# Attention and a squared-ReLU FFN in one kernel: fixed engine orders, and attention in pairs of chunks

## The chip, the cores and the metric

The kernel runs on one core of one Trainium2 chip. The metric is the device time of one execution in microseconds (us). The core has five engines that run side by side, each with a queue of its own that it works through in order: TensorE (PE, matrix products and transposes, into PSUM), VectorE (DVE), ScalarE (ACT), GpSimd (POOL), and SyncE (SP), which here issues all DMAs. [...]a bank holds 128 x 512 numbers of 32 bits.

## The reference

Sliding-window attention, whose result is the input of a feed-forward network (FFN):

```python
# q, k, v: [8, 8, 576, 64] (batch, head, position, head_dim), float32
scores = q @ k.transpose(0, 1, 3, 2) / 8
mask = (0 <= rel) & (rel < 64)              # rel = query position - key position
attn = softmax(where(mask, scores, -1e9))
x = (attn @ v).transpose(0, 2, 1, 3).reshape(4608, 512)
h = maximum(x @ w_in, 0)                    # w_in:  [512, 2048]
out = h * h @ w_out                         # w_out: [2048, 512]
```

## The kernel before

The 4608 tokens are cut into 36 chunks of 128 (two blocks of 64 positions, all eight heads), and the FFN into nine groups of four chunks (512 tokens). Everything that PE reads is 16-bit.

**A chunk of attention** has these steps:
- `load` (L176): three DMAs bring k, q and v in 32 bits into buffers of the pool `stage` (17 of them, shared with the weights), and POOL casts each one and makes a copy of v shifted by 64 partitions (L193 to L200).
- `transposes` (L202, chunks 0 to 11): PE transposes k and q into one PSUM bank, DVE copies k to `kT` (L213) together with a halo, the last 64 keys of the chunk before (L210), and ACT copies q to `qT` (L215). From chunk 12 on it is `transposes_k` (L218), and q is transposed by a DMA from SBUF to SBUF (L234).
- `scores` (L237): 16 small matmuls into two PSUM banks, one exponential on ACT and one minimum with a mask on DVE for each bank (L251, L253). The mask holds 65504 or 0, so the minimum keeps a value or clears it.
- `values` (L256): 16 matmuls for the two halves of the heads, each half into a bank of its own, with a reciprocal of the sum (L267) and a multiplication by it (L268) on DVE for each half.
- `to_xT` (L273): the result is transposed by PE and copied by DVE (chunks 0 to 11), or transposed by a DMA (L281, chunks 12 on).

**The FFN.** `ffn_up_chunk` (L326) computes h for one chunk in four quarters of w_in's columns (chunks 0 to 7). `ffn_up` (L309) does a group in 16 steps of four matmuls (L315), with a ReLU on ACT (L319) and the square on DVE (L320). `ffn_out` (L354) is the second product for group 0. `ffn_out_seven` (L373), for the groups 1 to 8, does it with seven half-size products in place of eight, in 14 steps, with sums of h on DVE (L387), and takes sums of w_out (L147 to L164).

**The order.** Work is handed out as a list of small steps. A front works through chunks 0 to 7 with their FFN (L446 to L467). Then comes a loop over g = 1 to 9 (L468): round g holds the output product of group g-1, the up product of group g, the attention of group g+1 and the loads of group g+2, mixed by `weave` (L16). A scheduler then orders the instructions of each engine by its own model of when they will be ready; only those given to `keep_in_program_order` (`pin`, L68), the loads and casts of the front, keep their order. The attention pool `ps_att` has four buffers of one bank.

Of the kernel before, what the change touches and what calls it, by code (L numbers as in the profile page):

```python
# [15 lines left out]
def weave(*streams):  # L16

    keyed = []
    for s, (steps, lo, hi) in enumerate(streams):
        n = len(steps)  # L20
        for i, step in enumerate(steps):
            keyed.append((lo + (hi - lo) * (i + 0.5) / n, s, i, step))
    keyed.sort(key=lambda e: e[:3])
    return [e[3] for e in keyed]
# [3 lines left out]
def kernel(  # L28
# [22 lines left out]
    NTB = NT // 512  # L51

# [12 lines left out]
    ps_att = ctx.enter_context(tc.tile_pool(name="ps_att", bufs=4, space=bass.MemoryType.PSUM))  # L65

    NFIRST = 8
    pin = tc.keep_in_program_order  # L68
# [3 lines left out]

# [10 lines left out]

    def make_mask(name, first):
        m = const.tile([P, HP * 2, 64], FP16, name=name)
        nc.vector.tensor_copy(out=m[:], in_=base[:].rearrange("p (o r) -> p o r", o=1)  # L90
                              .to_broadcast([P, HP * 2, 64]))
        m = m[:].rearrange("p (a b) r -> p a b r", b=2)
        if first is not None:
            nc.vector.memset(m[0:64, :, first, :], 0.0)
        return m

    mask_first = make_mask("mask_first", 0)
    mask_inner = make_mask("mask_inner", None)
    mask_second = make_mask("mask_second", 1)

    w_in_sb = const.tile([P, DMC, DFF], FP16, name="w_in_sb")
    w_out_sb = const.tile([P, FFC, DM], FP16, name="w_out_sb")

# [8 lines left out]
    def load_w_in():  # L112
        steps = []
        FQ = DFF // 4

        def one(quar, c):
            ws = stage.tile([P, FQ], FP32, name="ws", tag="st")
            pin(nc.sync.dma_start(out=ws[:], in_=moe_w_in[c * P:(c + 1) * P,
                                                          quar * FQ:(quar + 1) * FQ]))
            nc.vector.tensor_scalar(  # L120
                out=w_in_sb[:, c, quar * FQ:(quar + 1) * FQ], in0=ws[:],
                scalar1=W_SCALE, scalar2=None, op0=ALU.mult)

        for quar in range(4):
            for c in range(DMC):
                steps.append(lambda quar=quar, c=c: one(quar, c))
        return steps

    def load_w_out():
        def one(f):  # L130
            ws = stage.tile([P, DM], FP32, name="ws2", tag="st")
            pin(nc.sync.dma_start(out=ws[:], in_=moe_w_out[f * P:(f + 1) * P, :]))
            pin(nc.gpsimd.tensor_copy(out=w_out_sb[:, f, :], in_=ws[:]))

        return [lambda f=f: one(f) for f in range(FFC)]

    GW = 1
    GX = 3
    KH = FFC // 2
    NH = DM // 2
    wb = [const.tile([P, KH, NH], FP16, name=f"wb{i}") for i in range(3)]

    def w_out_sums():  # L147
        def sums(k0, kind):
            ks, kl = slice(k0, k0 + 2), slice(KH + k0, KH + k0 + 2)
            b11, b12 = w_out_sb[:, ks, 0:NH], w_out_sb[:, ks, NH:DM]  # L150
            b21, b22 = w_out_sb[:, kl, 0:NH], w_out_sb[:, kl, NH:DM]
            tt = nc.vector.tensor_tensor
            if kind == 0:
                tt(out=wb[1][:, ks], in0=b22, in1=b12, op=ALU.subtract)
            elif kind == 1:
                tt(out=wb[0][:, ks], in0=wb[1][:, ks], in1=b11, op=ALU.add)
            elif kind == 2:
                tt(out=wb[2][:, ks], in0=b21, in1=wb[0][:, ks], op=ALU.subtract)
            else:
                tt(out=b12, in0=b12, in1=b11, op=ALU.subtract)  # L160

        return ([lambda k0=k0, kind=kind: sums(k0, kind)
                 for kind in range(3) for k0 in range(0, KH, 2)],
                [lambda k0=k0: sums(k0, 3) for k0 in range(0, KH, 2)])  # L164


    xTs = {}
# [6 lines left out]
    q16s, k16s, qTs, kTs, pms, xs = {}, {}, {}, {}, {}, {}  # L174

    def load(i):  # L176

        pin = tc.keep_in_program_order if i < NFIRST else lambda ins: ins
        sts = []
        for (src, nm) in ((k, "k"), (q, "q"), (v, "v")):  # L180
            st = stage.tile([P, H, D], FP32, name=f"{nm}_st", tag="st")
            b0, j0 = divmod(2 * i, NB)
            if j0 + 1 < NB:
                pin(nc.sync.dma_start(
                    out=st[:], in_=src[b0, :, 64 * j0:64 * j0 + P, :].rearrange("h p d -> p h d")))
            else:
                pin(nc.sync.dma_start(
                    out=st[0:64], in_=src[b0, :, 64 * j0:S, :].rearrange("h p d -> p h d")))
                pin(nc.sync.dma_start(
                    out=st[64:P], in_=src[b0 + 1, :, 0:64, :].rearrange("h p d -> p h d")))  # L190
            sts.append(st)
        k16s[i] = st16.tile([P, H * D], FP16, name="k16", tag="k16")
        pin(nc.gpsimd.tensor_copy(out=k16s[i][:], in_=sts[0][:].rearrange("p h d -> p (h d)")))  # L193
        q16s[i] = st16.tile([P, H * D], FP16, name="q16", tag="q16")
        pin(nc.gpsimd.tensor_copy(out=q16s[i][:], in_=sts[1][:].rearrange("p h d -> p (h d)")))  # L195
        v_ev, v_od, v_next = v_evs[i % NV], v_ods[i % NV], v_ods[(i + 1) % NV]
        pin(nc.gpsimd.tensor_copy(out=v_ev[:, :, 0:D], in_=sts[2][:]))  # L197
        pin(nc.gpsimd.tensor_copy(out=v_od[64:P, :, 0:D], in_=v_ev[0:64, :, 0:D]))  # L198
        if i + 1 < NCK:
            pin(nc.gpsimd.tensor_copy(out=v_next[0:64, :, 0:D], in_=v_ev[64:P, :, 0:D]))  # L200

    def transposes(i):  # L202
        ps = ps_att.tile([P, 2, HP, P], FP16, name="qkT_ps", tag="ps_a")
        for s, src in enumerate((k16s, q16s)):
            for hp in range(HP):
                nc.tensor.transpose(out=ps[:, s, hp, :], in_=src[i][:, hp * P:(hp + 1) * P],
                                    identity=ident[:])
        kT = attw.tile([P, HP, 192], FP16, name="kT", tag="kT")
        if i > 0:
            nc.vector.tensor_copy(out=kT[:, :, 0:64], in_=kTs[i - 1][:, :, P:192])  # L210
        else:
            nc.vector.memset(kT[:, :, 0:64], 0.0)
        nc.vector.tensor_copy(out=kT[:, :, 64:192], in_=ps[:, 0])  # L213
        qT = attw.tile([P, HP, P], FP16, name="qT", tag="qT", bufs=8)
        nc.scalar.activation(out=qT[:], in_=ps[:, 1], func=AF.Copy, scale=1.0)  # L215
        kTs[i], qTs[i] = kT, qT

    def transposes_k(i):  # L218
        ps = ps_att.tile([P, HP, P], FP16, name="qkT_ps", tag="ps_a")
        for s, src in enumerate((k16s,)):  # L220
            for hp in range(HP):
                nc.tensor.transpose(out=ps[:, hp, :], in_=src[i][:, hp * P:(hp + 1) * P],
                                    identity=ident[:])
        kT = attw.tile([P, HP, 192], FP16, name="kT", tag="kT")
        if i > 0:
            nc.vector.tensor_copy(out=kT[:, :, 0:64], in_=kTs[i - 1][:, :, P:192])
        else:
            nc.vector.memset(kT[:, :, 0:64], 0.0)
        nc.vector.tensor_copy(out=kT[:, :, 64:192], in_=ps[:])
        kTs[i] = kT  # L230

    def transpose_q_dma(i):
        qT = attw.tile([P, HP, P], FP16, name="qT", tag="qT", bufs=8)
        nc.sync.dma_start_transpose(out=qT[:], in_=q16s[i][:])  # L234
        qTs[i] = qT

    def scores(i):  # L237
        sc = [ps_att.tile([P, HP, 2, 64], FP32, name=f"sc{hh}", tag="ps_a") for hh in range(2)]
        for hp in range(HP):
            for blk in range(2):  # L240
                for hh in range(2):
                    r0 = 64 * hh
                    nc.tensor.matmul(  # L243
                        sc[hh][:, hp, blk, :], kTs[i][r0:r0 + 64, hp, 64 * blk:64 * blk + P],
                        qTs[i][r0:r0 + 64, hp, 64 * blk:64 * blk + 64], start=True, stop=True)
        j0 = 2 * i % NB
        mask = mask_first if j0 == 0 else mask_second if j0 + 1 == NB else mask_inner
        pms[i] = []
        for hh in range(2):
            pm = attw.tile([P, HP, 2, 64], FP16, name=f"pm{hh}", tag=f"pm{hh}")  # L250
            nc.scalar.activation(out=pm[:], in_=sc[hh][:], func=AF.Exp,  # L251
                                 scale=1.0 / float(D) ** 0.5)
            nc.vector.tensor_tensor(out=pm[:], in0=pm[:], in1=mask, op=ALU.min)  # L253
            pms[i].append(pm)
# [193 lines left out]
    for s in w_in_steps[:12]:  # L448
        s()
# [63 lines left out]
```

The softmax here doesn't subtract the row's maximum and nothing guards it: scores larger than these inputs give would overflow.

## Time and profile before

| | |
|---|---|
| Median of three runs | 330.17 us (330.02 to 330.44) |
| Span of the profiled execution | 328.2 us |
| Mean granted TensorE clock | 0.987 |
| DMA: bytes moved, packets | 52.98 MB, 148199 |
| POOL waiting for the loads of k (L193) | 81.6 us, 15 waits |

The span runs from the first to the last instruction of one profiled execution; the runs' times contain a little more around it. A group of instructions is shown as line, engine, operation, output<-inputs, shape and count, then its busy time in us and the mean duration of one in ns, then the idle time of the engine just before and what ended it. The slices are 40 equal parts of the span, each digit the busy share in tenths. Durations of neighbouring instructions on one engine overlap, so the time from start to start is shorter than the duration.

### The profile page before, as it was taken

To read this page: it belongs to the slowest core of one execution; us is meant where nothing else is said; L and a number is where in the kernel's file an instruction comes from. 1 tells how busy PE (TensorE), PEld (TensorE's weight loads), DVE (VectorE), ACT (ScalarE), POOL (GpSimd) and SP (SyncE) were. 2 spreads that over 40 slices of the span, in tenths; PEclk is the share of its full clock that TensorE was granted. 3 is DMA by queue.
4 is the path that set the end of the run, shared out by engine and by line. 5 is a ranking of instruction groups with operands and counts; after the bars stand their busy time and mean duration, and the time that the engine had idled before them with its cause. 6 is when DMAs were issued, how large, how long until landed. Compare 5 with 4: busy or idle time off the path is not lost.

```text
span 328.2 us, 8415 instructions
## 1 busy us (share of the span) xinstructions
PE 302.5 (92%) x3334; PEld 205.7 (63%) x3334; DVE 274.7 (84%) x602; ACT 140.4 (43%) x249; POOL 132.6 (40%) x204
## 2 busy tenths in 40 slices
PE   1968989988999999999899999999999999999994
PEld 0357877864575667556565666666656666666683
DVE  2765988999988989898899899999989888876862
ACT  1243557543336543553355345535543544344310
POOL 5038898899907430564065446242822000000000
PEclk9996999999999999999999999999999999999999
DMA  7999989998929545976795788549954101300113
GB/s 196 331 236 222 234 247 373 221 229 208 224 59 248 134 92 155 221 140 132 186 231 113 167 230 187 92 101 277 202 131 115 66 19 32 139 7 2 64 66 128
DMA packets 148199, 52.98 MB, mean 161 GB/s; under 512 B 139456, under 2 KB 139456, under 8 KB 148160
## 3 DMA queue, kind: packets, MB, share of 16 engines
q1 hardware_dynamic: 148160, 52.45, 64.9%
q8 instruction: 26, 0.43, 0.5%
q14 instruction: 13, 0.11, 0.1%
HBM read 36.70 MB, written 9.44 MB: 141 GB/s over the span
## 4 chain that ended last, share of the span: by engine, by line
PE 64%; DVE 25%; ACT 4%; DMA 2%; issue 2%; SPq 2%; ACTq 0%; DVEq 0%
PE hps L315 25%; PE opsD L394 9%; PE opsC L394 8%; PE opsA L394 6%; DVE pm L253 5%; PE hps L336 4%; DVE h L341 4%; DVE h L320 4%; PE av L263 3%; PE opsB L394 3%; PE sc L243 2%; DMA ws<-in_moe_w_in_dram 2%; DVE h L387 2%; ACT hrelu L340 2%; DVE hs L387 2%
## 5 line engine op out<-in xcount | busy, mean ns | idle before, releaser
L315 PE MATMUL hps<-xT,w_in_sb 128*128 128x512 f16 x448 | 114.6, 380 | 3.3 <-DVE h L320 1.8
L319 ACT ACTIVATE hrelu<-hps 128x512 f32<-128x512 f32 x112 | 67.1, 599 | 104.6 <-PE hps L315 95.3
L320 DVE SCALAR_TENSOR_TENSOR h<-hps,hrelu 128x512 f16<-128x512 f32 x112 | 76.6, 684 | 20.7 <-ACT hrelu L319 19.5
L394 PEld LDWEIGHTS <-h 128*128 128x128 f16 x640 | 61.8, 98 | 19.0
L315 PEld LDWEIGHTS <-w_in_sb 128*128 128x128 f16 x448 | 40.7, 98 | 35.8 <-issue 3.3
L193 POOL CAST k<-k_st 128x512 f16<-128x512 f32 x36 | 24.7, 686 | 83.0 <-DMA k_st<-in_k_dram 81.6
L251 ACT ACTIVATE pm<-sc 128x512 f16<-128x512 f32 x72 | 39.0, 597 | 13.8 <-PE sc L243 13.8
L336 PE MATMUL hps<-xT,w_in_sb 128*128 128x128 f16 x512 | 37.8, 226 | 4.9 <-DVE h L341 1.6
L336 PEld LDWEIGHTS <-w_in_sb 128*128 128x128 f16 x512 | 32.1, 101 | 8.1 <-issue 4.6
L394 PE MATMUL opsD<-wb,h 128*128 128x256 f16 x256 | 32.9, 273 | 0.0
L394 PE MATMUL opsA<-w_out_sb,h 128*128 128x256 f16 x256 | 32.7, 273 | 0.0
L253 DVE TENSOR_TENSOR pm<-pm,mask_inner 128x512 f16<-128x512 f16 x56 | 29.7, 544 | 2.8 <-ACT pm L251 2.3
L195 POOL CAST q<-q_st 128x512 f16<-128x512 f32 x36 | 25.2, 699 | 13.4 <-DMA q_st<-in_q_dram 13.3
L340 ACT ACTIVATE hrelu<-hps 128x512 f32<-128x512 f32 x32 | 19.1, 598 | 26.6 <-PE hps L336 23.6
L197 POOL CAST v_ev<-v_st 128x512 f16<-128x512 f32 x36 | 23.5, 653 | 12.9 <-DMA v_st<-in_v_dram 12.2
L394 PEld LDWEIGHTS <-hs 128*128 128x128 f16 x256 | 23.8, 98 | 6.7 <-DVE hs L387 0.5
L268 DVE TENSOR_TENSOR x_sb<-av,rden 128x256 f16<-128x256 f32 x72 | 27.4, 416 | 0.1
L341 DVE SCALAR_TENSOR_TENSOR h<-hps,hrelu 128x512 f16<-128x512 f32 x32 | 21.9, 685 | 6.4 <-ACT hrelu L340 6.3
L200 POOL COPY v_od<-v_ev 64x512 f16<-64x512 f16 x35 | 25.0, 715 | 2.1
L198 POOL COPY v_od<-v_ev 64x512 f16<-64x512 f16 x36 | 24.2, 673 | 2.3
L263 PEld LDWEIGHTS <-pm 128*64 128x64 f16 x576 | 12.9, 110 | 13.4 <-issue 5.7
L263 PE MATMUL av<-v_od,pm 128*64 128x65 f16 x288 | 18.0, 198 | 2.1 <-DVE pm L253 1.4
(63 smaller groups left out, 349.0 us busy)
## 6 DMA issues: line engine op xcount, KB each, us to landing
k_st<-in_k_dram SPq DMA_DIRECT2D x32, 256.0 KB, 3.9
q_st<-in_q_dram SPq DMA_DIRECT2D x32, 256.0 KB, 4.2
v_st<-in_v_dram SPq DMA_DIRECT2D x32, 256.0 KB, 4.4
out_dram<-osb SPq DMA_DIRECT2D x16, 512.0 KB, 3.0
ws<-in_moe_w_in_dram SPq DMA_DIRECT2D x16, 256.0 KB, 5.9
ws<-in_moe_w_out_dram SPq DMA_DIRECT2D x16, 256.0 KB, 5.6
k_st<-in_k_dram SPq DMA_DIRECT2D x8, 128.0 KB, 2.9
q_st<-in_q_dram SPq DMA_DIRECT2D x8, 128.0 KB, 3.1
```

Of the source, the lines that this page charges most:

```text
L195: pin(nc.gpsimd.tensor_copy(out=q16s[i][:], in_=sts[1][:].rearrange("p h d -> p (h d)")))
L251: nc.scalar.activation(out=pm[:], in_=sc[hh][:], func=AF.Exp, scale=1.0 / float(D) ** 0.5)
L253: nc.vector.tensor_tensor(out=pm[:], in0=pm[:], in1=mask, op=ALU.min)
L263: nc.tensor.matmul(av[64 * blk:64 * blk + 64, h % 4, 0:65], pms[i][h % 2][:, h // 2, blk, :], vv[:, h, 0:65], start=True, stop=True)
L268: nc.vector.tensor_tensor(out=x_sb[:, 4 * half:4 * half + 4, :], in0=av[:, :, 0:D], in1=rden[:].to_broadcast([P, 4, D]), op=ALU.mult)
L315: nc.tensor.matmul(hps[:], w_in_sb[:, c, f * P:(f + 1) * P], xT_of(g)[:, c, :], start=(c == 0), stop=(c == DMC - 1))
L319: nc.scalar.activation(out=hrelu[:], in_=hps[:], func=AF.Relu)
L320: nc.vector.scalar_tensor_tensor(out=h2s[g][:, f, :], in0=hps[:], scalar=0.0, in1=hrelu[:], op0=ALU.max, op1=ALU.mult)
L336: nc.tensor.matmul(hps[:, f, :], w_in_sb[:, c, (4 * fq + f) * P:(4 * fq + f + 1) * P], xT_of(g)[:, c, t0:t0 + P], start=(c == 0), stop=(c ...
L340: nc.scalar.activation(out=hrelu[:], in_=hps[:], func=AF.Relu)
L341: nc.vector.scalar_tensor_tensor(out=h2s[g][:, 4 * fq:4 * fq + 4, t0:t0 + P], in0=hps[:], scalar=0.0, in1=hrelu[:], op0=ALU.max, op1=ALU.mult)
L394: nc.tensor.matmul(banks[bank][:, m, :], a[:, k, m * P:(m + 1) * P], w[:, k], start=(first and k == 0 and m == 0), stop=(k == KH - 1), ski ...
```

## The change

All instructions are now issued in program order on every engine (`manual_schedule`). For chunks 0 to 11 and the first FFN group that order comes from a table of some 440 words. Each word is a step: `fk3` fetches k of chunk 3, `kc`, `qc`, `vc`, `vd` cast and shift, `T` transposes, `S` scores, `e` exponential, `m` minimum, `V` values, `n` normalises, `X`/`x` transposes and copies the result, `U2.1` is quarter 1 of the up product of chunk 2 with `r` and `s` its ReLU and square, `fw`/`w` fetch and scale pieces of w_in, `fo`/`o` those of w_out, `O` is the output product, `ws` sums of w_out, `tk`/`tq` transposes by DMA, `h` a halo, `W` matmuls that only keep PE warm.

```diff
+Q_ACT = (0,)
+FIRST = '''
+fk0 fq0 fv0 fw0.0 fw0.1 kc0 fw0.2 qc0 fw0.3 fk1 T0 W4 vc0 fq1 ck0 cq0 vd0 fv1 w0.0 S0 W6 w0.1 ea0
+fw1.0 w0.2 eb0 ma0 mb0 w0.3 V0 W5 fw1.1 kc1 n0 fw1.2 qc1 fw1.3 X0 fk2 T1 x0 vc1 fq2 U0.0 cq1 ck1
...
+ws2.2 oe0 st0 ws2.3 qc11 X9 tk11 O1.1 x9 vc11 vd11 O1.2 tq11 S10 O1.3 e10 h12 fk12 O2.0 fq12 oe1
+st1 m10 fv12 S11 fk13 V10 e11 O2.1 n10 fq13 kc12 O2.2 m11 fv13 qc12 X10 V11 x10 O2.3 n11 tk12 vc12
+vd12 O3.0 oe2 st2 tq12 X11 kc13 O3.1 x11 qc13 tk13 O3.2 vc13 vd13 O3.3 tq13 oe3 st3 fk14 fq14 fv14
...
+'''
...
-    ps_att = ctx.enter_context(tc.tile_pool(name="ps_att", bufs=4, space=bass.MemoryType.PSUM))
-    pin = tc.keep_in_program_order
+    ps_att = ctx.enter_context(tc.tile_pool(name="ps_att", bufs=2, space=bass.MemoryType.PSUM))
+    ctx.enter_context(tc.manual_schedule())
```

The masks are now made before any weight piece is scaled. The w_in pieces of one quarter of the columns (four of them) are fetched between the chunks 0 to 3, where before twelve came after chunk 0 and four after chunk 1. The cast of q of chunk 0 is on ACT. The up products of single chunks take the banks of two pools in turn. In the front, the output product of group 0 comes after the last up product of group 1.

Attention uses buffers of two banks. One exponential, one minimum, one reciprocal and one multiplication serve a whole chunk:

```diff
+    def att_bank(name, dtype=FP32):
+        return ps_att.tile([P, 2, 512], FP32, name=name, tag="ps_a")
...
+    def expo(i, part=slice(0, 2)):
+        nc.scalar.activation(out=pms[i][:, part], in_=scs[i][:, part], func=AF.Exp,
+                             scale=1.0 / float(D) ** 0.5)
+
+    def keep(i, part=slice(0, 2)):
...
+        nc.vector.tensor_tensor(
+            out=pms[i][:, part], in0=pms[i][:, part],
+            in1=mask[:].rearrange("p (o a) r -> p o (a r)", o=1)
+            .to_broadcast([P, part.stop - part.start, 512]), op=ALU.min)
...
+    def norm(i):
+        xs[i] = attw.tile([P, 2, HP, D], FP16, name="x_sb", tag="x_sb")
+        rden = smallp.tile([P, 2, 4, 1], FP32, name="rden", tag="rden")
+        nc.vector.reciprocal(out=rden[:], in_=avs[i][:, :, :, 64:65])
+        nc.vector.tensor_tensor(
+            out=xs[i][:], in0=avs[i][:, :, :, 0:D],
+            in1=rden[:].to_broadcast([P, 2, 4, D]), op=ALU.mult)
```

`kT` holds a pair of chunks, so there is one halo for two chunks. From chunk 8 on k and q are both transposed by DMA on SP. The result x is transposed by PE for chunks 0 to 15 and by DMA from 16 on:

```diff
+    def halo(i):
+        p = i // 2
+        if p == 0:
+            nc.vector.memset(kT_of(0)[:, :, 0:64], 0.0)
+        else:
+            nc.vector.tensor_copy(out=kT_of(p)[:, :, 0:64], in_=kT_of(p - 1)[:, :, 2 * P:2 * P + 64])
...
+    def dma_kT(i):
+        nc.sync.dma_start_transpose(out=k_cols(i), in_=k16s[i][:])
```

The rounds g = 2 to 9 place their steps by fractions of the round: 14 steps of the output product evenly, 16 of the up product evenly from 0.05 on, and the attention of two chunks at a time. A minimum is issued two steps (`tick`) after its scores. The up product keeps its three operations (`UP` is `ffn_up` unchanged):

```diff
+        for h in range(2):
+            a, b, t = c + 2 * h, c + 2 * h + 1, 0.46 * h + (0.1 if g == 3 else 0.0)
+            ev += [(t + 0.02, lambda a=a: sc(a)), (t + 0.021, lambda b=b: sc(b)),
+                   (t + 0.25, lambda a=a: va(a)), (t + 0.251, lambda b=b: va(b)),
+                   (t + 0.36, lambda a=a: to_xT(a)), (t + 0.361, lambda b=b: to_xT(b))]
...
+        for h in range(2):
+            t = 0.48 * h
+            for n in range(2):
+                i = c + 2 * h + n
+                if i < NCK:
+                    ev.append((t + 0.06 + 0.05 * n, lambda i=i: (dma_kT(i), dma_qT(i))))
+                if i < NCK and n == 0:
+                    ev.append((t + 0.2, lambda i=i: halo(i)))
+                if i + 2 < NCK:
+                    ev.append((t + 0.14 + 0.18 * n, lambda i=i: load(i + 2)))
...
+    for g in range(2, NTB + 1):
+        if g == 2:
+            for k0 in range(0, KH, 2):
+                w_out_sum(k0, 3)
+        ev = even(out_seven(g - 1))
+        if g < NTB:
+            ev += [(0.05 + 0.95 * t, s) for t, s in even([lambda f=f: UP(g, f) for f in range(FFC)])]
         if g + 1 < NTB:
+            ev += attention(g + 1)
+            ev += loads(4 * g + 6)
+        for _, s in sorted(ev, key=lambda e: e[0]):
             s()
```

In `loads`, c is 4g+6: a round transposes the second pair of group g+1 and the first pair of group g+2, and loads the two pairs after these.

## The prediction

> **What bounds the kernel now.** I read four views, in this order. The page's head gives the shares and the slices:
> ```profile
> PE 302.5 (92%) x3334; PEld 205.7 (63%) x3334; DVE 274.7 (84%) x602; ACT 140.4 (43%) x249; POOL 132.6 (40%) x204
> PE   1968989988999999999899999999999999999994
> DVE  2765988999988989898899899999989888876862
> DMA  7999989998929545976795788549954101300113
> ```
> TensorE (PE) is full from about 110 us on, VectorE (DVE) is close behind, and DMA is full until about 90 us and loose later. So the kernel has a front, held by data and by waits, and a loop held by PE with DVE beside it. The stretches of the loop (start to end in us, then busy us and count of each engine):
> ```profile
> core 0: us, PE busy (x) PEld busy (x) DVE busy (x) ACT busy (x) POOL busy (x), PEclk, DMA share, GB/s
> 192.00:224.00 32.00, 32.00 (x330) 20.62 (x329) 29.84 (x64) 15.05 (x27) 13.62 (x19) 1.00 0.68 157
> 224.00:255.00 31.00, 30.72 (x321) 19.95 (x320) 28.68 (x62) 14.45 (x26) 13.01 (x19) 1.00 0.71 170
> 285.00:312.00 27.00, 27.00 (x188) 18.17 (x186) 19.27 (x31) 11.24 (x19) 0.00 (x0) 1.00 0.11 39
> ```
> DVE is busy 93% of a round with attention, 71% of the one without. The first product of each round (bank opsA, PE's timeline) starts at 92.3, 127.7, 159.7, 193.3, 224.0, 255.1, 285.5 and 310.7: the front is 92.3 long, the six rounds g=2..7 take 193.2 (35.4, 32.0, 33.6, then 30.7 on average), round 8 takes 25.2, and from there it is 17.5 to the end of the span at 328.2. Third, the operations that the change touches (mean ns is of one, overlap with the next included):
> ```profile
> L253 DVE TENSOR_TENSOR pm<-pm,mask_inner 128x512 f16<-128x512 f16 x56 | 29.7, 544 | 2.8 <-ACT pm L251 2.3
> L268 DVE TENSOR_TENSOR x_sb<-av,rden 128x256 f16<-128x256 f32 x72 | 27.4, 416 | 0.1
> L229 DVE COPY kT<-qkT_ps 128x512 f16<-128x512 f16 x24 | 9.9, 414 | 0.7 <-PE qkT_ps L222 0.4
> L267 DVE RECIPROCAL rden<-av 128x4 f32<-128x4 f32 x72 | 9.4, 164 | 2.2 <-PE av L263 2.2
> L226 DVE COPY kT<-kT 128x256 f16<-128x256 f16 x24 | 7.4, 312 | 0.1
> L222 PE MATMUL qkT_ps<-ident,k 128*128 128x128 f16 x96 | 9.4, 219 | 0.0
> ```
> Last, the start. PE's first FFN matmul is at 18.30, because DVE, in its order, holds the masks and the k copy behind the first weight piece:
> ```profile
> 7.05 0.43 DVE L120 TENSOR_SCALAR w_in_sb<-ws 128x512 f16<-128x512 f32 x1 [5.16 <-DMA ws<-in_moe_w_in_dram]
> 9.48 0.42 DVE L213 COPY kT<-qkT_ps 128x512 f16<-128x512 f16 x1
> 18.30 1.95 PE L336 MATMUL hps<-xT,w_in_sb 128*128 128x128 f16 x32 [0.52 <-DVE xT L278]
> ```
>
> **What the Trainium skill says.** "VectorE: DVE Perf Modes", section "The TRN2 errata", says that an operation pays a fixed cost per instruction, so one large tile pays it once. The trace agrees: a 128x256 f32 read from PSUM takes 416 ns (L268), the 128x512 one at L410 682 ns; doubling adds 266 and not 416. "SBUF — State Buffer", section "SBUF: two separate sides", says that DVE operations with two SBUF inputs and GpSimd take a shared port pair in turn. The trace agrees: the mask minimum is 544 ns over the run, but 423 in the window 250 to 285, where POOL is idle. "DMA: Bandwidth & Descriptors", section "Rules for kernel authors", says that a transpose needs nothing special beside ordinary DMAs. Here a transpose lands 2.4 to 2.7 us after issue, but holds SP's sequencer for 1.19 us, twice a load's 0.57.
>
> **Part 1, the settled round.** From the chain: four up matmuls take 0.86 us, eight output matmuls 0.87. With 16 and 14 such groups that is 26.0 us. From PE's timeline, start to next start: scores 0.34, values 0.38, four k transposes 0.22 a chunk. Before: 26.0 + 4 x 0.94 = 29.8, measured 30.7; 0.9 is left for switches (up groups beside attention take 0.97 instead of 0.86) and waits for DVE. After: the k transposes leave PE, 4 x 0.22 = 0.9. Two scores, and two values, stand side by side, so half the switches go: I estimate 0.5 left. Sum 26.0 + 2.9 + 0.5 = 29.4. In-order DVE queues then cost something: a square behind two minima (1.3) or two norms (1.4) can be late for the next but one up group, which has about 1.5 us of slack (two up periods of 1.84, less 0.86 matmul, 0.6 relu, 0.6 square). Bounds 0 and 1.6 a round; I take 0.5, since DVE gets lighter. Round: 29.9.
>
> DVE per chunk before: two minima at a pitch of 0.34 to 0.55, two reciprocals 0.16, two products 0.67, k copy 0.33, halo 0.2: about 2.2. After: one minimum 0.62 (the 128x1024 f16 sums of L387 take 0.69 without POOL), one reciprocal 0.09, one product 0.60, half a halo 0.1: 1.4. That is 3.2 us a round, and DVE falls from 28.7 to about 25. This gives nothing of its own; it pays for the stall term. ACT's two exponentials (1.08 a pair) become one of about 0.95, hidden, as ACT is under half busy.
>
> What the k transposes cost instead: 4 more a round. In the window 262 to 272 the DMA share 0.11 with 0.26 MB is two transposes, so 0.55 us of all 16 engines each: the share goes from 0.70 to about 0.77. SP holds 12 x 1.21 + 12 x 0.57 + 2 x 0.39 = 22.1 of 29.9. Both fit. Behind a waiting transpose on SP stand the loads two pairs ahead and the x transposes. Issued at 0.06 and 0.11 of a round (3.3 us) and done by 3.3 + 4 x 1.2 + 2.7 = 11, they are wanted at 0.48 (14.4): some 3 us to spare. Cost taken: 0, bounds 0 and 2.7 (one landing) a pair.
>
> Round 2 has the x transposes of chunks 12 to 15 back on PE (0.9) and four weight sums on DVE ahead of its first squares (2.3 us, of which I let 0.5 show): 31.3. Six rounds: 31.3 + 5 x 29.9 = 180.8. This holds rounds 3 and 4 to be as settled as the later ones. Before they were 2 to 3 longer, and round 2 nearly 5, with attention left over from the front in it (x transposes still at 95 to 98 us) and DVE full; the table ends that attention within the front. If they stay long, it is up to 5 more, which the range takes in.
>
> **Part 2, the front.** By PE: chunk 0 no longer waits behind weights, and its first quarter is enough for U0.0. Casts end at about 5.4; T0, copies, warm, S0, exponential, minimum, V0, X0 (with the durations of the timeline) end near 13, five us sooner. But S2 stands in PE's order ahead of U1.0, and chunk 2 is the 15th to 17th transfer, at about 1 us each near 19: so at 22 us PE has done two of 32 quarter steps. Left then: 30 x 1.07 = 32.1, five T at 0.45 (2.2), nine S (3.1), ten V (3.8), ten X (2.2), the output products of group 0, 64 x 0.216 = 13.8: 57.2. The granted clock was 0.81 and 0.84 between 20 and 40 us, which I count again as 2.5, and 3 for waits: 84.7. Before, O was laid among the U steps; now it comes last, with four PSUM banks for the U steps, and DVE's front load falls by 12 x 0.8.
>
> By DMA: before, chunk 11 had landed at 71.5 (its v cast starts without a wait), with 17.9 MB moved. Now eight transposes stand ahead, 0.55 to 1.2 each (5 to 10), and SP waits twice for casts before it can issue the next loads (about 1 each, unknown, 0 to 4). So S11 runs near 79, and behind it on PE stand V10, V11, X10, X11 and seven quarter products, 0.34 + 1.2 + 6.1 = 7.6: 87. Chunks 12 and 13 follow behind the stores st1 to st3, about 3 us into round 2, about when they are wanted. I take the larger, 87; bounds 83 and 93. Before: 92.3.
>
> **Part 3, the end.** Round 8 at 26.0 (25.2 before), and the last one, whose first B product still waits for two sums behind the last square, 16.8 with the last store: 42.8 against 42.7.
>
> **Sum.** 87 + 180.8 + 42.8 = 310.6, to be set beside the span 328.2. The runs' median of 330.17 is 2.0 over that span, so 312.6. Five us come from the front and twelve from the rounds.
>
> **Rivals.**
> - A, PE at its floor. No stall in the rounds, the front as PE has it: 83 + 30.3 + 5 x 29.4 + 42.8 + 2 = 305. For it: DVE gets 3 us of room. Against it: order is fixed on every engine, and no wait can be stepped around.
> - B, the fixed order eats the fusing. Only two attention buffers, each of two banks, and in-order queues leave rounds at 31.0, and only the long first ones gain; the front stays at 92.3, held by loads and transposes: 92.3 + 6 x 31 + 42.8 + 2 = 323. For it: DMA is full in the front, and PE already shows no idle time that can go. Against it: the k transposes do leave PE.
> - C, slower. S heads PE's queue while its k or q transpose is late: SP is 74% held, and one late cast on POOL holds all that follows. Each pair then costs PE up to a landing, 2.7 us; two pairs in six rounds are 32 us, about 345. It decides from (330.2 - 2 - 87 - 42.8) / 6 = 33.1 a round, that is 1.5 us a pair. Against it: about 3 us of lead and loads two pairs ahead.
> - That the change does not do what it says: the tables fix orders and not times, so this is B.
>
> **Chances.** Forecast 0.50, A 0.16, B 0.18, C 0.14, no change 0.02. Of the outcomes 303 to 327 holds the forecast, B and most of A; C and a little of A are left out. About 0.2% is what a measurement of this kernel can tell from no change. Faster 0.84, within 0.2% 0.02, slower 0.14.
>
> **What would show it.** Round starts (first opsA product) 29 to 30.5 apart show part 1 right; 31 or more speaks for B. The first product of round 2 at 84 to 90 shows the front. A wait of PE's scores for a kT or qT transpose of over 1 us in the rounds is C. The DVE share should fall to about 78%, and the k copies at L229 vanish. I am wrong if the two-bank minimum costs over 1.1 us, or if PE idles over 1.5 us a round behind DVE.

## The result, and the profile after

The changed kernel takes 334.29 us (median of four runs, 330.98 to 334.79), the kernel before 330.1 us on the same chip: a ratio of 1.0102, 95% interval 1.0053 to 1.0151. It is slower by about 1%. Some executions of a kernel are in a slower state, and all ratios here are of the others alone, while the medians are of all executions. The profiled execution has a span of 332.5 us, 4.3 more than before.

The head of the page of the changed kernel:

```profile
PE 293.1 (88%) x3215; PEld 199.1 (60%) x3215; DVE 247.1 (74%) x454; ACT 138.5 (42%) x212; POOL 135.4 (41%) x203
PE   4768789949879999899699999999999899999984
DVE  3476698976486888978757979778877878776663
PEclk9959599997999999999879999999999999999999
DMA  7899899979979699894989797779789730400213
```

The groups of the new minimum and product (line, operation, busy us and mean ns of one, idle before):

```profile
L272 DVE TENSOR_TENSOR pm<-pm,mask_inner 128x1024 f16<-128x1024 f16 (+1 forms) x29 | 23.5, 811 | 4.2 <-ACT pm L266 4.2
L292 DVE TENSOR_TENSOR x_sb<-av,rden 128x512 f16<-128x512 f32 x36 | 24.9, 691 | 1.2
```

They took 29.7 and 27.4 us before. What the change was to take away, it took: PE is busy 9.4 us less than before, DVE 27.6 us less. And yet the span is longer, so the time is in PE's gaps: the span less PE's busy time is 39.4 us, against 25.7 before. A slice is 8.3 us. PE's slices show three places: the 7, 6 and 7 in the first 42 us, the 4 at 66 to 75 us with the 7 at 91 to 100, and the 6 at 158 to 166. PEclk is below 9 in or just after most of them.

The first product of each round (bank opsA) now starts at 94.8, 128.5, 160.2, 196.4, 226.4, 257.2, 288.1 and 314.1. Two of these stretches, and the round without attention, in the table by window (columns as before):

```profile
core 0: us, PE busy (x) PEld busy (x) DVE busy (x) ACT busy (x) POOL busy (x), PEclk, DMA share, GB/s
160.20:196.40 36.20, 32.38 (x312) 19.99 (x304) 26.42 (x43) 14.45 (x23) 18.30 (x27) 0.91 0.93 187
196.40:226.40 30.00, 29.33 (x310) 19.01 (x304) 24.66 (x43) 14.41 (x23) 12.94 (x19) 1.00 0.80 188
288.10:314.10 26.00, 26.00 (x177) 17.21 (x176) 18.71 (x30) 10.77 (x18) 0.00 (x0) 1.00 0.11 41
```

The undisturbed round takes 30.0; the one before it 36.2, with the clock at 0.91 and 3.8 us in which PE is not busy. The waits name who was late (engine and line that waited, whom for, us in total, times, longest):

```profile
PE sc L259 <- DMA qT<-q: 7.7, 4, 2.3
...
PEld L347 <- DMA xT<-x_sb: 4.4, 2, 3.5
```

Both are transposes by DMA, issued by SP. The trace of the kernel before has no wait of PE for either. PE's timeline at 160 us shows what one of them does (start, duration, instruction, in brackets the idle time before):

```profile
160.24 1.05 PE L415 MATMUL opsA<-w_out_sb,h 128*128 128x256 f16 x8
164.53 1.86 PE L347 MATMUL hps<-xT,w_in_sb 128*128 128x512 f16 x4 [3.25 <-DVE hs L408]
166.19 1.91 PE L415 MATMUL opsA<-w_out_sb,h 128*128 128x256 f16 x8
167.90 1.91 PE L347 MATMUL hps<-xT,w_in_sb 128*128 128x512 f16 x4
```

The bracket names DVE, whose sum `hs` ended at 164.37; the line of the waits has PE's weight load at the same place waiting 3.5 us for `xT`, and the second transpose of the pair, issued at 162.07, landed at 164.44. Edit 1 below decides between the two. In it the transposes are issued 5 us sooner, and the same matmul starts 2.5 us before that sum ends:

```profile
161.91 1.03 PE L347 MATMUL hps<-xT,w_in_sb 128*128 128x512 f16 x4
163.43 0.98 DVE L408 TENSOR_TENSOR hs<-hs,h 128x1024 f16<-128x1024 f16 x1
```

So it was the transpose. After the wait the matmuls take 1.86 to 1.91 us where they took 1.05, and a wait of 3.25 us costs about 6: this round against the next.

Why the transpose was late stands in SP's own timeline:

```profile
152.45 1.21 SPq L248 DMA_TRANSPOSE qT<-q  x1
153.71 0.66 SPq L111 DMA_DIRECT2D k_st<-in_k_dram  x1
...
159.09 1.15 SPq L108 DMA_DIRECT2D v_st<-in_v_dram  x1
160.35 2.93 SPq L311 DMA_TRANSPOSE xT<-x_sb  x2
```

`x_sb` of this pair was ready at 154.6. The transposes stand in the queue behind nine loads (those of two chunks, one of them in halves), whose data is wanted much later, and SP has no pause between 152 and 163 us. Added up over the round from 196.4 to 226.4, SP issues 12 transposes (16.1 us, 1.34 each) and 15 other DMAs (12.4 us, 0.83 each): 28.4 of 30.0 us, with no pause of over 0.2 us between two of them. In the kernel before it was 21.5 of 30.8, in the round from 193.3 on.

In the front it is similar. SP is issuing 85.7 of 94.8 us (73.6 of 92.3 before), and the four new transposes of a pair hold up the loads behind them:

```profile
62.54 3.14 SPq L108 DMA_DIRECT2D v_st<-in_v_dram  x1
65.86 1.49 SPq L245 DMA_TRANSPOSE kT<-k  x1
67.46 1.19 SPq L248 DMA_TRANSPOSE qT<-q  x1
68.74 1.22 SPq L245 DMA_TRANSPOSE kT<-k  x1
70.12 1.19 SPq L248 DMA_TRANSPOSE qT<-q  x1
71.37 1.79 SPq L108 DMA_DIRECT2D k_st<-in_k_dram  x1
```

PE's timeline shows the scores of chunks 8, 9 and 13 waiting for them:

```profile
69.83 0.41 PE L259 MATMUL sc<-qT,kT 64*128 64x64 f16 x16 [2.30 <-DMA qT<-q]
...
74.29 0.41 PE L259 MATMUL sc<-qT,kT 64*128 64x64 f16 x16 [2.16 <-DMA qT<-q]
...
100.02 0.41 PE L259 MATMUL sc<-qT,kT 64*128 64x64 f16 x16 [2.15 <-DMA qT<-q]
```

### The profile page after: what moved, and what is told of

Its sections match the earlier page's. It is cut to its first block, busy times and chain, and to the rows that moved or that the text cites. A ratio compares the mean times of both kernels' runs of the same rounds, so it can differ in the third digit from the quotient of the medians.

```text
span 332.5 us, 8072 instructions
## 1 busy us (share of the span) xinstructions
PE 293.1 (88%) x3215; PEld 199.1 (60%) x3215; DVE 247.1 (74%) x454; ACT 138.5 (42%) x212; POOL 135.4 (41%) x203
## 2 busy tenths in 40 slices
DMA packets 163429, 56.63 MB, mean 170 GB/s; under 512 B 154688, under 2 KB 154688, under 8 KB 163392
## 3 DMA queue, kind: packets, MB, share of 16 engines
q1 hardware_dynamic: 163392, 56.12, 73.6%
## 4 chain that ended last, share of the span: by engine, by line
PE 49%; DMA 15%; DVE 14%; POOL 7%; issue 5%; ACT 4%; SPq 4%; POOLq 0%
PE hps L347 22%; PE opsC L415 7%; PE opsD L415 6%; PE opsA L415 5%; DMA v_st<-in_v_dram 4%; DVE hs L408 4%; DMA ws<-in_moe_w_in_dram 4%; DVE pm L272 4%; PE opsB L415 3%; SPq L108 3%; DVE h L352 3%; PE av L284 3%; ACT pm L266 2%; ACT hrelu L351 2%; DMA qT<-q 2%
## 5 line engine op out<-in xcount | busy, mean ns | idle before, releaser
L352 DVE SCALAR_TENSOR_TENSOR h<-hps,hrelu 128x512 f16<-128x512 f32 x112 | 76.2, 688 | 38.3 <-ACT hrelu L351 38.1
L415 PEld LDWEIGHTS <-h 128*128 128x128 f16 x640 | 62.4, 98 | 21.5 <-issue 0.6
L347 PEld LDWEIGHTS <-w_in_sb 128*128 128x128 f16 x448 | 42.4, 98 | 44.9 <-issue 8.7
L266 ACT ACTIVATE pm<-sc 128x1024 f16<-128x1024 f32 (+1 forms) x38 | 35.7, 977 | 14.5 <-PE sc L259 14.3
L329 PE MATMUL hps<-xT,w_in_sb 128*128 128x128 f16 x512 | 34.9, 228 | 3.3 <-DVE w_in_sb L189 3.0
L329 PEld LDWEIGHTS <-w_in_sb 128*128 128x128 f16 x512 | 31.5, 103 | 4.7 <-DVE w_in_sb L189 3.7
L415 PE MATMUL opsA<-w_out_sb,h 128*128 128x256 f16 x256 | 33.8, 277 | 0.0
L415 PEld LDWEIGHTS <-hs 128*128 128x128 f16 x256 | 24.8, 99 | 13.8 <-DVE hs L408 5.9
L180 POOL CAST v_ev<-v_st 128x512 f16<-128x512 f32 x36 | 25.4, 706 | 13.3 <-DMA v_st<-in_v_dram 12.9
L184 POOL COPY v_od<-v_ev 64x512 f16<-64x512 f16 x36 | 25.9, 719 | 2.3
L272 DVE TENSOR_TENSOR pm<-pm,mask_inner 128x1024 f16<-128x1024 f16 (+1 forms) x29 | 23.5, 811 | 4.2 <-ACT pm L266 4.2
L292 DVE TENSOR_TENSOR x_sb<-av,rden 128x512 f16<-128x512 f32 x36 | 24.9, 691 | 1.2
L186 POOL COPY v_od<-v_ev 64x512 f16<-64x512 f16 x35 | 25.0, 714 | 2.0
L259 PE MATMUL sc<-qT,kT 64*128 64x64 f16 x576 | 13.0, 192 | 8.6 <-DMA qT<-q 7.7
L415 PE MATMUL opsB<-wb,hs 128*128 128x256 f16 x128 | 17.1, 277 | 3.1 <-DVE hs L408 3.1
```

What stands on the lines that cost most here:

```text
L180: nc.gpsimd.tensor_copy(out=v_evs[i % NV][:, :, 0:D], in_=sts["v", i][:])
L266: nc.scalar.activation(out=pms[i][:, part], in_=scs[i][:, part], func=AF.Exp, scale=1.0 / float(D) ** 0.5)
L272: nc.vector.tensor_tensor(out=pms[i][:, part], in0=pms[i][:, part], in1=mask[:].rearrange("p (o a) r -> p o (a r)", o=1) .to_broadcast([P, ...
L292: nc.vector.tensor_tensor(out=xs[i][:], in0=avs[i][:, :, :, 0:D], in1=rden[:].to_broadcast([P, 2, 4, D]), op=ALU.mult)
L329: nc.tensor.matmul(hps[:, f, :], w_in_sb[:, c, (4 * fq + f) * P:(4 * fq + f + 1) * P], xT_of(g)[:, c, t0:t0 + P], start=(c == 0), stop=(c ...
L347: nc.tensor.matmul(hps[:], w_in_sb[:, c, f * P:(f + 1) * P], xT_of(g)[:, c, :], start=(c == 0), stop=(c == DMC - 1))
```

## The experiments

Four theories stood against each other. Q, or H: SP's queue is full, and what stands at its head (in H, a store that waits for PE) holds what PE waits for. D: the transfers themselves are too much for the DMA engines. W: the fixed order costs time, because no engine can step around a wait. F: the operations on two banks bring little. All kernels are edits of the changed one. Ratios are against the kernel before, timed on the same chip; the changed kernel stands at 1.0102. The texts put in below call the edits 1, 2 and 6 `e1_x_first`, `e2_pe_8_11` and `e6_stores_late`.

| edit | median us | ratio | 95% interval |
|---|---|---|---|
| 1 loads behind the x transposes | 328.98 | 0.996 | 0.9931 to 0.999 |
| 2 chunks 8 to 11 transposed by PE | 328.83 | 0.9993 | 0.997 to 1.0016 |
| 3 k by PE in the rounds | 336.34 | 1.0207 | 1.0172 to 1.0242 |
| 4 one operation per bank | 335.12 | 1.0151 | 1.0109 to 1.0193 |
| 5 order by the scheduler | 342.96 | 1.044 | 1.0385 to 1.0495 |
| 6 edit 1, stores later | 329.23 | 1.0 | 0.998 to 1.0021 |
| 7 edits 1, 2, stores later | 323.2 | 0.9822 | 0.9782 to 0.9863 |
| 8 edit 1, w_in as before | 327.5 | 0.9932 | 0.9909 to 0.9956 |
| 9 edit 7, w_in as before | 323.85 | 0.9829 | 0.9796 to 0.9862 |
| 10 edit 7, one operation per bank | 332.24 | 1.0083 | 1.005 to 1.0117 |
| 11 edits 1 and 2 | 324.44 | 0.9835 | 0.9798 to 0.9872 |
| 12 edit 7 once more | 323.48 | 0.9822 | 0.9784 to 0.9859 |

**Edit 1.** In the rounds, the loads are put behind the x transposes:

```diff
-                    ev.append((t + 0.14 + 0.18 * n, lambda i=i: load(i + 2)))
+                    ev.append((t + 0.14 + 0.26 * n, lambda i=i: load(i + 2)))
```

> Only the place of every second load in the rounds moves: from 0.32 and 0.80 of a round to 0.40 and 0.88, so that on SP it stands behind the two x transposes and no longer ahead of them. Theory Q (SP's queue is full, and transposes behind loads hold PE): the waits of the first up matmul for xT (3.5 us at 164, 1.6 at 260, 0.6 at 228) vanish, with the slow clock after the first; the round starting at 160 falls from 36.2 to about 30.5, the time by 6 to 8 us to about 327. Theory W (two attention buffers and engines in fixed order hold PE): no change beyond 1 us, 334.

The rounds from 161 us on take 30.6, 31.0, 31.0 and 29.9, and the round of 36.2 is gone. But the scores of chunk 13 now wait 3.30 us at 98.13, with slow matmuls after it: the front ended 3.2 us sooner, at 91.5, and their data only 1.9 us sooner. Round 2 takes 38.1 us for it, against 33.7. The edit does not touch the front, so the 3.2 us are a difference between two executions (edit 3, with the same front, ends it at 93.4). Only a part of the loss is in the rounds after it.

**Edit 2.** The table's k and q transposes of the chunks 8 to 11 go back to PE, each ahead of an up or output product:

```diff
-... X7 tk8 ... o15 tq8 s6.1 U7.0 ... tk9 ... tq9 ... U7.2 ...
+... X7 ... o15 s6.1 T8 ck8 cq8 U7.0 ... T9 ck9 cq9 U7.2 ...
-... tk10 ... tq10 O1.0 ... tk11 ... tq11 ...
+... T10 ck10 cq10 O1.0 ... T11 ck11 cq11 O1.2 ...
```

> Chunks 8 to 11 have k and q transposed by PE again, as chunks 0 to 7; all else as after. Theory Q: eight transposes at about 1.4 us each leave SP in the front, loads go out earlier, the waits of scores for qT (2.3, 2.2, 1.1 and 2.2 us) shrink; first product of round 2 at 89 to 91 and not 94.8; time 4 to 6 us less, about 329. Theory W: PE gets 4 x 0.45 more, 336. If data alone limits the front (rival D), the loads of chunk 11 land as late as before and the gain is under 2 us.

The front ends at 92.3 and the waits of the chunks 8 and 9 are gone; the waits for x transposes in the rounds are still there (1.27, 0.65 and 2.37 us), and chunk 13 waits 1.63 us at 97.66, again with slow matmuls after it. By their ratios the edits 1 and 2 are worth 1.4% and 1.1%, in different places.

**Edit 3.** k is transposed by PE in the rounds as well, in one of the two-bank buffers, and copied by DVE:

```diff
-                    ev.append((t + 0.06 + 0.05 * n, lambda i=i: (dma_kT(i), dma_qT(i))))
+                    ev.append((t + 0.06 + 0.05 * n, lambda i=i: dma_qT(i)))
+                    ev.append((t + 0.31 + 0.05 * n, lambda i=i: Tk(i)))
```

> In the rounds k is transposed by PE, with a copy by DVE, for chunks 14 to 35; q and x stay with DMA. PE gets 22 x 0.22 = 4.8 us, DVE 22 x 0.33, SP loses 22 transposes of about 1.4. Theory Q: SP busy falls from 29 to about 24 us a round, waits for xT vanish, rounds at about 31 each: about 4.8 more and 7 less, 332. Theory W: 4.8 more and nothing less, 339 or above.

No x transpose is late any more, but rounds 3 to 6 take 31.6 to 32.2: PE's transpose waits 11 times, 5.5 us in all, until DVE has freed one of the two buffers. Together these four rounds take 127.5 us, against 128.7 in the changed kernel and 123.9 in edit 1, where k stays on SP and only the order is changed. What makes edit 3 slower than the changed kernel is round 2 (40.2 us against 33.7), in which chunk 13's scores wait 3.83 us. So in the rounds SP is the better place for k with these buffers, if its order is right; in the front, by edit 2, it is the worse one.

**Edit 4.** Exponential, minimum, reciprocal and product are each two operations of one bank again:

```diff
-            S_(i)
-            expo(i)
-            later(2, lambda: keep(i))
+            S_(i)
+            expo(i, lo)
+            expo(i, hi)
+            later(2, lambda: (keep(i, lo), keep(i, hi)))
```

> The two-bank exponential, minimum, reciprocal and product are each done as two operations of one bank; orders, buffers and transposes as after. DVE gets about 36 x 0.3 = 11 us more, ACT 36 x 0.1. Theory Q: DVE has room, so the time stays within 1.5 us of 334. Theory W: the stalls behind DVE grow, 3 to 6 us more, 338.

The interval overlaps that of the changed kernel, so here the operations on two banks show no clear worth. DVE is busy 13.8 us more (260.9), and PE waits 10.2 us for squares, against 3.6. In part the small difference is luck: in its profiled execution the wait for `xT` at 163.97 was 2.53 us and no slow matmul followed, so that round 4 takes 34.4 and not 36.2, while rounds 3, 5 and 6 take 0.9 to 2.0 us more than in the changed kernel. That the waits for squares seemed to cost so little was the reason for edit 10.

**Edit 5.** The order is left to the scheduler again:

```diff
-    ctx.enter_context(tc.manual_schedule())
```

> The changed kernel with the fixed order taken away: the same steps in the same program text, but the scheduler orders each engine's instructions again. Theory Q: SP has the same 12 transposes and 12 loads a round to issue, so SP stays full; what changes is who stands behind whom: 326 to 336, about that of the changed kernel (334). Theory W (fixed orders are what costs): 3 to 10 us less than the changed kernel, below the kernel before (329).

3% slower than with the fixed order. W falls as far as this tests it: the order by the table and by fractions gains time on the scheduler with these operations. A scheduler with the loads and casts of the front pinned, as in the kernel before, was not tried.

**Edit 6.** Edit 1, and the stores `st0` to `st2` of the first output products go behind the last transpose of chunk 13:

```diff
-... oe0 st0 ... oe1 st1 ... oe2 st2 tq12 ... tq13 oe3 st3 ...
+... oe0 ... oe1 ... oe2 tq12 ... tq13 st0 st1 st2 oe3 st3 ...
```

> As e1_x_first, and the stores of the first three token blocks stand behind the transposes of chunk 13 on SP and no longer between the loads. Theory Q, with SP busy without a break from 62 to 100 us: the stores wait little there, so chunk 13's scores come 1 to 3 us earlier (95 to 97 and not 98.1); time 1 to 2 us under e1_x_first. If a store that waits for PE holds the loads back in itself (theory H, head of the line), 4 us or more.

No gain over edit 1: chunk 13 still waits 2.40 us at 98.01. With the eight transposes in front of it, the loads of chunk 12 are issued from 82.13 us on (85.84 in the changed kernel, 72.00 in edit 12).

**Edit 7.** Edits 1, 2 and 6 together.

> e1_x_first, e2_pe_8_11 and e6_stores_late together. In e2_pe_8_11 SP stood still from 73 to 81 us at the first store, whose data PE had not made, with the loads of chunks 12 and 13 behind it. Theory H: with no transposes and no store ahead of them these loads go out at 73 to 80 us, the scores of chunk 13 no longer wait, round 3 starts at 121 to 124 and not 128; with e1's rounds 7 or 8 us under the kernel before, ratio 0.975 to 0.98. If DMA bandwidth limits the front (rival D), round 3 starts at 126 or later and the ratio stays at 0.99.

Faster than both kernels. No wait of PE for a transpose by DMA of 0.5 us or more is left, the loads of the chunks 12 and 13 are issued between 72.6 and 81 us, round 3 starts at 123.3, and the rounds take 31.5, 31.4, 30.8, 31.1, 31.4 and 30.2. The ratio is a little above the range that H expected. The bytes are nearly those of the changed kernel (55.58 against 56.63 MB), and so is the DMA share (73.0% against 73.6%). D falls: it was the order and the time of issue, not the amount.

**Edit 8.** Edit 1, with twelve w_in pieces ahead of chunk 1 and four behind it, as before:

```diff
-fk0 fq0 fv0 fw0.0 fw0.1 kc0 fw0.2 qc0 fw0.3 fk1 T0 ... fw1.0 ... fw1.1 ... fw1.2 ... fw1.3 ...
+fk0 fq0 fv0 fw0.0 fw0.1 fw0.2 fw0.3 fw1.0 ... fw2.3 fk1 fq1 kc0 qc0 fv1 T0 ... fw3.0 ... fw3.3 ...
```

> As e1_x_first, but w_in is fetched as in the kernel before: twelve pieces ahead of chunk 1 and four behind it, orders on all other engines kept. If w_in between the chunks is worth what it was taken to be worth, the first FFN matmul is at 17 to 19 us and not 13.6, and the time is 2 to 4 us over e1_x_first. If data limits the front later on anyway (chunk 13's transposes), the time is the same within 1 us.

Not slower than edit 1; PE waits 5.69 us at 17.92 for k of chunk 1. The front ends at 93.1, against 91.5, but round 3 starts 2.1 us sooner than in edit 1.

**Edits 9 to 12** were timed on one chip. Edit 12 is edit 7 unchanged, and stands beside the other three.

> The three mends of SP's order (loads behind the x transposes, k and q of chunks 8 to 11 on PE, three stores behind the fetches of chunk 13) with the twelve w_in pieces fetched ahead of chunk 1, as the kernel before had them. Theory 'the quarters of w_in between the chunks are worth nothing': within 2 us of the kernel with the three mends, 321 to 325 us. Rival 'the early start counts once SP is free': the first FFN product comes some 5 us later, and the run ends 3 to 5 us later, 326 to 328 us.

The first FFN product comes at 20.04 instead of 13.17 (edit 12), and the time is the same to 0.4 us. The early start that the quarters bring is worth nothing that these runs can tell.

> The three mends of SP's order, with exponential, minimum, reciprocal and product again one for each bank. Theory 'DVE's fixed cost per instruction counts once SP does not hold the rounds': PE waits more for DVE, rounds 32 and more, against 31.1, and 327 to 331 us. Rival 'DVE has room': within 1.5 us of the kernel with the three mends, 322 to 325 us.

8.8 us slower than edit 12 beside it, and the intervals are far apart. In edit 10 against edit 12 the two groups, and PE's wait for squares. First edit 12 (line, operation, busy us and mean ns of one, idle before):

```profile
L274 DVE TENSOR_TENSOR pm<-pm,mask_inner 128x1024 f16<-128x1024 f16 (+1 forms) x29 | 22.8, 786 | 6.5 <-ACT pm L268 6.4
L294 DVE TENSOR_TENSOR x_sb<-av,rden 128x512 f16<-128x512 f32 x36 | 24.9, 691 | 1.2
```

and edit 10:

```profile
L274 DVE TENSOR_TENSOR pm<-pm,mask_inner 128x512 f16<-128x512 f16 x56 | 31.2, 588 | 2.9 <-ACT pm L268 2.7
L296 DVE TENSOR_TENSOR x_sb<-av,rden 128x256 f16<-128x256 f32 x72 | 30.5, 424 | 2.5
```

The waits of edit 12 have this line:

```profile
PE hps L349 <- DVE h L354: 4.1, 9, 0.8
```

and those of edit 10 this one:

```profile
PE hps L351 <- DVE h L356: 12.5, 21, 1.6
```

One bank at a time, a minimum takes 588 ns and not half of 786, a product 424 and not half of 691. (The comparison in the prediction was of operations that read PSUM; the minimum reads SBUF.) DVE is busy 14.5 us more, its squares are late, and the six rounds from the end of the front to round 8 take 194.4 us instead of 185.7. F falls: the operations on two banks are worth 8.8 us once SP's queue is in order. Why edit 4 shows so little of it beside the changed kernel is not shown beyond the round named there.

> Two of the three mends: loads behind the x transposes, k and q of chunks 8 to 11 on PE; the stores st0 to st2 stay where the change put them, ahead of the loads of chunks 12 and 13. Theory 'a store in SP's queue holds the loads behind it': SP stands still until the first output product is stored, the scores of chunk 13 wait over 1.5 us, and 326 to 328 us. Rival 'only the transposes counted': 322 to 324.5 us, as with all three.

The median is 1 us from that of edit 12, inside both intervals, so the stores' place is not shown to count by the ratio; the transposes in the front and the order of the loads in the rounds carry the gain, from 1.0102 to 0.9835. But two of the six executions took 328.69 and 330.08 us and are not in the ratio, and the second of them is the profiled one. It shows what the theory about the stores said:

```profile
72.09 0.91 SPq L110 DMA_DIRECT2D v_st<-in_v_dram  x1
81.95 0.36 SPq L394 DMA_DIRECT2D out_dram<-osb  x1
82.41 0.39 SPq L110 DMA_DIRECT2D k_st<-in_k_dram  x1
```

SP stands for 9 us at the first store, and the scores of chunk 13 wait 1.62 us. Whether the other four executions had this wait too, and if so why they lost nothing by it, stays open.

> The kernel with the three mends once more, unchanged, beside the other three on the same chip, with five rounds. If its gain over the kernel before is real, the ratio lies between 0.978 and 0.987 again, and the whole interval below 0.99.

The ratio is the same again, 0.9822, with an interval that ends at 0.9859. What SP does in it at the place of the long wait:

```profile
145.51 0.66 SPq L113 DMA_DIRECT2D k_st<-in_k_dram  x1
...
148.92 0.63 SPq L115 DMA_DIRECT2D v_st<-in_v_dram  x1
149.65 2.56 SPq L313 DMA_TRANSPOSE xT<-x_sb  x2
152.31 0.52 SPq L438 DMA_DIRECT2D out_dram<-osb  x1
152.89 0.46 SPq L110 DMA_DIRECT2D k_st<-in_k_dram  x1
153.40 2.21 SPq L110 DMA_DIRECT2D q_st<-in_q_dram  x1
```

Three of the nine loads now stand behind the x transposes, which are issued 5 us before the round of PE that needs them (it starts at 154.9). In the changed kernel they were issued at 160.35, as that round began. SP is no less full: in the rounds that start at 154.9, 185.5 and 216.7 its instructions last 27.9, 28.8 and 27.9 us, and the rounds take 30.6, 31.2 and 30.7. So the full queue by itself does not set the round; what stands ahead of what in it does.

## Why the prediction was wrong

The predicted time was 312.6 us, the span under it 310.6; it came to 332.5. The 21.9 us between them lie as follows.

| part | forecast | changed kernel | edit 12 |
|---|---|---|---|
| front | 87 | 94.8 | 92.0 |
| rounds 2 to 7 | 180.8 | 193.3 | 185.7 |
| from round 8 to the end | 42.8 | 44.4 | 44.4 |
| span | 310.6 | 332.5 | 322.1 |

The last column is the changed kernel with SP's queue mended: 10.4 us of the error go with SP's queue, and 11.5 are sizes of other terms. These are single executions. By the ratios the mending is worth 2.8%, some 9 us, and of the three parts the front is the least sure: its 2.8 us are within the 3.2 us by which the changed kernel and edit 1 differ there with the same front. The mending also gave PE the transposes of four chunks.

**The step that failed** is the one on SP in part 1: "SP holds 12 x 1.21 + 12 x 0.57 + 2 x 0.39 = 22.1 of 29.9. Both fit." and, from it, "Cost taken: 0". The count of DMAs was right but for one, the prices were not. The means of the kernel before, in its round from 193.3 on, were already 1.23 us for a transpose and 0.76 for a load or store, on a queue with pauses. In the changed kernel, with the DMA share at 0.80, a transpose holds SP for 1.34 us on average and a load or store for 0.83, and SP is held 28.4 of 30.0 us. Then the "some 3 us to spare", reckoned from an issue at 0.06 of a round, do not exist, because a full queue is late by what stands ahead in it. The step did name the x transposes behind the waiting transpose, and then checked only the k and q of the next pair. It was the x transposes, behind nine loads, that were late: by 3.25 us in the round from 160.2 on, which took 36.2 and not 29.9. Edit 1 removed that by order alone, and edit 12 shows that a queue just as full does no such harm. The Trainium skill, "DMA: Bandwidth & Descriptors", section "Issuing engines are not separate DMA queues", says that the time to initiate a DMA is usually small beside the DMA itself. Here the mean of 0.83 us for a load or store stands beside medians of 4.1 to 4.4 us from issue to landing of the loads, and 27 DMAs of a round fill the issuing engine; the measurement decides.

**The second half of that step, in part 2.** "Chunks 12 and 13 follow behind the stores st1 to st3 [...] about when they are wanted": chunk 13 was 2.15 us late, and 3.30 late as soon as the front ended sooner. The eight transposes were counted at 5 to 10 us against the loads, which was of the right size (two pairs of four took 5.5 and 7.8 us from the first issue to the end of the last), but as a delay of S11 and not of the loads of the chunks 12 and 13, which stand in the same queue.

**What was not in the sum: the clock after a wait.** The forecast counted 2.5 us of it, for the front between 20 and 40 us, as before. A wait can bring its own, as that of 3.25 us did, though not each does (last section). Removing that wait in edit 1 shortened that round by 5.6 us, from 36.2 to 30.6.

**Sizes that were off without SP.** Rounds 3 to 7 of edit 12 take 30.8 on average and not 29.9: the term for what DVE has late, taken as 0.5 within bounds of 0 and 1.6, is about 1.4. PE is busy 29.3 to 29.6 us in rounds 3 to 6, which is the sum without that term (29.4), and over rounds 3 to 7 it waits 3.2 us for squares and 4.3 us for the sums `hs` of the output product, 1.5 a round. The prediction had the squares and not these sums, and over 1.5 of idling behind DVE was one of its own signs of being wrong. Edit 10 shows that DVE does set this: with more DVE work PE waits 10.3 us for squares in these rounds, and they grow. Round 8 came to 26.0, as said, and what follows it to 18.4, not 16.8. The front of edit 12 is 92.0: three waits of together 2.2 us for w_in pieces at 32 to 34 us, one of 3.27 us for chunk 1's minimum at 18.03 and one of 2.15 us for a minimum at 59.69 are 7.6 us where the sum by PE has "3 for waits", and the clock is at 0.5, 0.7 and 0.7 in the slices with them. These were not tried one by one.

**What was right.** DVE got lighter by 27.6 us; its share, forecast at "about 78%", is 77% in edit 12 and 74% in the changed kernel's longer span. The first FFN product came at 13.58, where the working had near 13. One start was misread, 159.7 for 159.3, which changes nothing. The undisturbed round of the changed kernel took 30.0 against 29.9, and "DVE gets lighter" does pay for the stall term: without it, in edit 10, rounds 3 to 7 take 32.3 on average. That the quarters of w_in lead to little, since "at 22 us PE has done two of 32 quarter steps", was read rightly, though not priced as nothing: edit 9 shows no difference. The fixed order, which rival B charged, gains on the scheduler instead (edit 5).

**Of the rivals**, B has the numbers of the mended kernel: a front of 92.3, rounds of 31.0 and 323, where edit 12 has 92.0, 31.0 and 323.5. That is luck: B had the front held by loads and transposes, and edit 12 takes eight transposes out of it. C named the place for the front: scores at the head of PE's queue behind a late transpose. Its price of 2.7 us a pair was near (2.30, 2.16, 2.15), but it happened to four chunks of the front and of round 2 (7.7 us), not in every round, and its point of decision, 33.1 a round, was reckoned with a front of 87 and an end of 42.8. With the front and the end as they came, (330.2 - 2 - 94.8 - 44.4) / 6 = 31.5 a round is enough to lose; the rounds were 32.2 on average. It reckoned with SP at 74%; it was at 95%.

## What to carry to other kernels

Count the issuing queue as an engine: take mean durations of its instructions from the busiest stretch, not the shortest ones, and when the sum comes near the round, look at the order within it. A queue held for 28.8 of 31.2 us did no harm in edit 12 once its order was right. Put what is wanted first ahead of what is fetched for later; with the queue's order changed and four chunks taken off it, the same kernel went from 1.0102 to 0.9822. And test a part's worth in a kernel whose other waits are gone: the operations on two banks showed no clear worth beside SP's waits (1.0151 against 1.0102, with intervals that overlap), and 8.8 us without them.

## What the runs showed of the hardware

**TensorE at half speed after a pause.** After the 3.25 us wait four matmuls took 1.86 us instead of about 1.03. The changed kernel shows it at the start as well, before and after a wait of 3.59 us:

```profile
13.58 1.05 PE L329 MATMUL hps<-xT,w_in_sb 128*128 128x128 f16 x16
...
18.79 0.26 PE L284 MATMUL av<-v_od,pm 128*64 128x65 f16 x1 [3.59 <-DVE pm L272]
...
20.00 1.89 PE L329 MATMUL hps<-xT,w_in_sb 128*128 128x128 f16 x16
```

and edit 5 after one of 4.39 us (1.86 again). The Trainium skill, "TensorE: Matmul & The Clock Gate", section "What's actually happening", tells of half the clock after an idle window of about 3.4 us. The factor agrees. Here shorter waits were followed by slow matmuls too: 2.76 us in edit 7 (1.89 us for 16 of the same matmuls), 2.30 with 2.16 us close to each other in the changed kernel, and in edit 2 one of 1.63 us, with 0.50 us shortly before it:

```profile
97.66 0.41 PE L261 MATMUL sc<-qT,kT 64*128 64x64 f16 x16 [1.63 <-DMA qT<-q]
98.00 1.89 PE L349 MATMUL hps<-xT,w_in_sb 128*128 128x512 f16 x4
```

In edit 12, a single one of 2.15 us at 59.69 was followed by 32 matmuls in 3.06 us, where the changed kernel has 1.96. Others were not: 2.82 us in edit 8, 2.53 in edit 4, 2.40 in edit 6, and in the changed kernel those of 2.15 us at 100.02 and of 1.59 at 259.87. So among waits of under 3 us in these runs the length alone does not decide; what does was not tried.

**A transpose by DMA holds SP.** It is never under 1.19 us, in the kernel before too, and 1.3 to 1.6 on average in rounds 2 to 6 of the changed kernel, with a DMA share of 0.79 to 0.93. Its loads of k and q have medians of 0.62 and 0.63 us, those of v 0.85, and the longest shown took 3.14, in the front.
